# The up products of the last block as seven products of halves, on four streams and eight banks

## Chip, cores and metric

The kernel runs on one core of a Trainium2 chip. The metric is the device time of one execution in microseconds (us), as the median of several runs. The engines named below are PE (TensorE, matmuls; PEld is its weight load), DVE (VectorE), ACT (ScalarE), POOL (GpSimd) and SP (SyncE, which here only issues DMAs).

## What is computed

An attention with normalised queries and keys, followed by a gated feed-forward block (SwiGLU):

```python
q_n, k_n = rmsnorm(q, g_q), rmsnorm(k, g_k)        # 8 batches, 12 heads, 448 tokens, 64 wide
attn = softmax(q_n @ k_n.T / 8)
x = (attn @ v), heads side by side                 # 3584 x 768
g, val = x @ w_gate, x @ w_val                     # both 768 x 1536
out = (silu(g) * val) @ w_out                      # 1536 x 768
```

All of it is float32. The change touches only `x @ w_gate` and `x @ w_val`, the "up" products, of a quarter of the tokens.

## The kernel before

**Blocks and stages.** The eight batches are taken two at a time, as four blocks, `n` = 0 to 3. A block has an up stage (gate and value products), then a down stage (the product with `w_out`). Attention of the next block's tokens is interleaved with the down stage of blocks 0 to 2; block 3 has no attention beside it.

**Fifteen products.** A block's `x` is seen as 2 x 3 blocks (two batches, three thirds of the 768 columns), and a weight as 3 x 3 blocks. Their product is done with 15 block products instead of 18. Each product `x` of `UP_ORDER` needs one sum of `x` blocks (kept in the tile `xs`, two 128-row chunks of 448 tokens, made by `sides`, L1191) and one sum of weight blocks (made once by `convert` and kept in DRAM as `up_sides`, loaded as `ws` by `load_sides`, L1417). The products go to five chains, and each is read from PSUM as soon as it is done: by a copy on ACT (COPY, L1409) or an addition or subtraction on DVE (L1411 to L1415) into one of six running sums `t0`, `t1`, `d`, `t3`, `t4`, `t5`. `UP_READ` says which; a third entry names the outcome (0 to 5) which that read completes. The outcomes are completed at steps 7, 10, 11, 12, 13 and 14 of the 15.

**Groups.** The up stage of a block has four groups `g` (a quarter of the hidden width each). A group is 15 steps, a step is a gate product and a value product (`which` = 0 and 1), a product is two chunks of 128 rows with 448 columns. In the profile each float32 matmul shows as two records, so a product is four records and a group 120. Gate products use the two PSUM banks `mm`, value products the two banks `at`, in turn. When an outcome is complete, ACT takes silu of the gate (`gate`, L1551, from SBUF `gt` into a PSUM tile `st`), and DVE multiplies by the value (`weigh`, L1554, back into `gt`). The product with `x` = 0 is followed by one more DVE sum, `add_d` (L1528).

**The down stage** has 15 products as well, each of two halves `s` over all four groups (L1663). `combine` (L1612) makes their operands from `gt`: products 6 and 1 come first and their operands, in the tile `hs`, are made group by group (L1185 and L1189 `hs`), after outcomes 0, 1 and 4 of that group. The third product's operand is one wide sum over all groups (L1185, 1792 columns).

**The order of the work** is made when the program is built: every piece is added to a list with an engine, a duration, a due time `when`, a `rank`, the pieces that it comes after, and the buffers that it takes or uses. `Order.run` (L432) then takes, for each free engine, the piece with the smallest key `when - rank` among those that can start first. On the chip each engine runs its pieces in the order so fixed, and waits on semaphores. PSUM reads have rank 60, `combine` has rank 0 and is due when its group ends. Pieces marked `port` (sums of SBUF operands on DVE and POOL) are laid one after the other. `read`, `emit` and the like are the closures that issue a piece. `begin[g]` in the change is the due start of group `g`.

The lines that set the edge between the up and the down stage:

```python
for g in range(NG):
    when = start + 30 * (g + 1) * unit + 1.0
    before = [down_done.get(n - 1)] + ([staged[HS]] if n == 0 else [])
    combine(6, a1, a2, None, when, [hidden[g, 0], hidden[g, 1], *before], g)
    combine(1, b2, h0, ALU.subtract, when, [made[6][g], hidden[g, 4], *before], g)
combine(10, h1, b1, None, block_end(n) + 3.0, [*all_hidden, *made[1], up_done[n]])
```

## Time and profile before

| | |
|---|---|
| median of 3 runs | 1455.47 us (1453.88 to 1456.11) |
| span of the profiled execution, first to last instruction | 1452.0 us |
| up stage of block 3 | 1173.8 to 1354.2 us |
| down stage of block 3 | 1354.2 to 1444.6 us, then the last reads and stores |
| HBM traffic | 157.29 MB read, 34.60 MB written |

The profile comes from one execution of its own; only its span is known, and the runs are measured apart from it. A row of the windows view has the stretch in us, its length, then for PE, PEld, DVE, ACT and POOL the busy us and the number of records, then the granted clock of TensorE (1.00 is full), the share of the DMA engines that is busy, and GB/s. A row of the timeline has start, length (of several merged records where it ends in x and a number above 1), engine, line, operation, the tiles written and read, and in brackets the idle time before it with what ended it. A row of the groups view has line, engine, operation, tiles, shapes and count, then busy us and mean ns of one, then the idle time before them. A row of the chain of work that ended last has start, length, engine, tile, line and count.

### The profile page before, as it was taken

What the parts mean: (1) busy time and instruction counts of PE and PEld (TensorE: products, weight loads), DVE (VectorE), ACT (ScalarE), POOL (GpSimd) and SP (SyncE); (2) the same over time, 40 slices, a digit from 0 to 9 for tenths busy, and PEclk for the clock granted to TensorE, in tenths of its full rate; (3) what the DMA queues carried; (4) which work ended last, traced back from release to release, by engine and by line L of the source; (5) the groups of instructions that cost most, each with busy time, mean ns of one, the idle gap of its engine ahead of it and who ended that gap; (6) DMA issues with size and microseconds to landing.
All of it is one profiled execution on the core that took longest, in us unless ns stands there. A gap on an engine that the chain in (4) does not pass through costs nothing.

```text
span 1452.0 us, 19362 instructions
## 1 busy us (share of the span) xinstructions
PE 1426.0 (98%) x6736; PEld 689.5 (47%) x6736; DVE 879.8 (61%) x1485; ACT 601.6 (41%) x1210; POOL 405.7 (28%) x476
## 2 busy tenths in 40 slices
PE   8999999999999999999999999999999999999997
PEld 4455454534444455544444455544444445555553
DVE  5889876878866434546877642455686644442533
ACT  6875444476653222356564122345555322212100
POOL 4756666625443000022443200011434300000000
PEclk9999999999999999999999999999999999999999
DMA  7778979854643533433644623443463452322235
GB/s 196 217 219 268 352 266 310 260 149 90 129 103 64 133 102 92 114 113 70 122 98 86 138 74 107 107 112 93 85 126 77 95 135 73 108 73 90 69 100 110
DMA packets 410416, 193.29 MB, mean 133 GB/s; under 512 B 280004, under 2 KB 390852, under 8 KB 410308
## 3 DMA queue, kind: packets, MB, share of 16 engines
q1 hardware_dynamic: 399040, 190.57, 49.1%
q10 hardware_dynamic: 11140, 1.38, 0.7%
q8 instruction: 55, 0.90, 0.3%
q14 instruction: 53, 0.43, 0.1%
q0 software_dynamic: 128, 0.00, 0.0%
HBM read 157.29 MB, written 34.60 MB: 132 GB/s over the span
## 4 chain that ended last, share of the span: by engine, by line
PE 90%; DMA 3%; DVE 2%; ACT 2%; SPq 1%; issue 1%; POOL 1%; ACTq 0%; DVEq 0%; POOLq 0%
PE at L1474 25%; PE mm L1474 25%; PE mm L1663 23%; PE at L1049 8%; PE st L970 7%; PE st L1080 1%; PE mm L1080 1%; DMA out_dram<-spare 1%; SPq L768 1%; DMA work<-in_k_dram 1%; ACT es L985 1%; DMA xs<-in_moe_w_gate_dram 0%; PE st L908 0%; DMA v<-in_v_dram 0%; ACT work L918 0%
## 5 line engine op out<-in xcount | busy, mean ns | idle before, releaser
L1474 PE MATMUL at<-xs,ws 128*128 128x448 f32 x960 | 401.2, 540 | 2.5 <-DVE v L1413 1.4
L1474 PE MATMUL mm<-xs,ws 128*128 128x448 f32 x960 | 401.7, 541 | 0.2 <-DVE hs L1315 0.2
L1474 PEld LDWEIGHTS at<-xs,ws 128*128 128x128 f32 x960 | 181.4, 190 | 184.7 <-issue 166.7
L1474 PEld LDWEIGHTS mm<-xs,ws 128*128 128x128 f32 x960 | 182.2, 190 | 180.7 <-issue 177.9
L888 POOL TENSOR_TENSOR work<-work,rr 128x448 f32<-128x448 f32 x72 | 71.8, 1016 | 467.5 <-DVE rr L715 341.6
L1663 PE MATMUL mm<-gt,ws 128*128 128x448 f32 x448 | 175.5, 543 | 0.0
L970 PE MATMUL st<-work 64*64 64x448 f32 (+1 forms) x1536 | 151.2, 501 | 10.3 <-ACT work L918 4.9
L985 ACT ACTIVATE es<-st 128x896 f32<-128x896 f32 x129 | 114.2, 914 | 101.6 <-PE at L1049 87.8
L1411 DVE TENSOR_TENSOR gt<-gt,mm 128x448 f32<-128x448 f32 x64 | 39.7, 621 | 188.1 <-PE mm L1474 161.7
L1663 PE MATMUL mm<-hs,ws 128*128 128x448 f32 x384 | 151.3, 544 | 0.0
L990 POOL TENSOR_TENSOR sums<-es 128x896 f32<-128x896 f32 x36 | 77.2, 2145 | 176.8 <-PE st L1080 83.7
L1663 PEld LDWEIGHTS mm<-gt,ws 128*128 128x128 f32 x448 | 83.6, 190 | 83.0 <-issue 80.8
L1551 ACT ACTIVATE st<-gt 128x448 f32<-128x448 f32 x96 | 52.3, 547 | 159.1 <-DVE gt L1415 85.7
L1409 ACT COPY gt<-mm 128x448 f32<-128x448 f32 x80 | 42.6, 532 | 157.5 <-PE mm L1474 157.4
L1049 PE MATMUL at<-es,v 64*64 64x448 f32 (+1 forms) x1032 | 106.0, 507 | 0.0
L1663 PEld LDWEIGHTS mm<-hs,ws 128*128 128x128 f32 x384 | 71.3, 190 | 71.0 <-issue 70.1
L970 PEld LDWEIGHTS st<-work 64*64 64x64 f32 x1536 | 50.9, 133 | 79.1 <-issue 37.4
L1409 ACT COPY v<-at 128x448 f32<-128x448 f32 x96 | 51.0, 532 | 80.4 <-PE at L1474 79.6
L990 POOL TENSOR_TENSOR sums<-sums,es 128x896 f32<-128x896 f32 x36 | 76.0, 2112 | 2.8
L1049 PEld LDWEIGHTS at<-es,v 64*64 64x64 f32 (+1 forms) x1032 | 44.1, 134 | 56.2 <-issue 50.4
L1554 DVE SCALAR_TENSOR_TENSOR gt<-st,v 128x448 f32<-128x448 f32 x96 | 59.7, 622 | 7.3 <-DVE v L1415 0.5
L1411 DVE TENSOR_TENSOR v<-v,at 128x448 f32<-128x448 f32 x64 | 39.8, 621 | 39.6 <-PE at L1474 39.5
(170 smaller groups left out, 1550.5 us busy)
## 6 DMA issues: line engine op xcount, KB each, us to landing
ws<-up_sides SPq DMA_DIRECT2D x32, 1024.0 KB, 5.6
ws<-down_sides SPq DMA_DIRECT2D x16, 1024.0 KB, 5.7
ws<-down_sides SPq DMA_DIRECT2D x28, 512.0 KB, 4.8
ws<-up_sides SPq DMA_DIRECT2D x16, 768.0 KB, 4.9
out_dram<-spare SPq DMA_DIRECT2D x168, 56.0 KB, 2.1
v<-in_v_dram SPq DMA_DIRECT2D x96, 96.0 KB, 2.5
ws<-up_sides SPq DMA_DIRECT2D x32, 256.0 KB, 5.9
ws<-up_sides SPq DMA_DIRECT2D x16, 512.0 KB, 5.8
```

The costliest lines, as they stand in the source:

```text
L888: nc.gpsimd.tensor_tensor(out=tiles["t", m][:, x], in0=tiles["qk", (m, x)], in1=rr.to_broadcast([P, NC, C]), op=ALU.mult,)
L970: nc.tensor.matmul(st[ds(D * x, D), h, 0:n], tiles["KT", m][rows, ds(P * j + D * of_keys, D)], tiles["QT", m][rows, ds(Q * of_queries, n)] ...
L985: nc.scalar.activation(e, tiles["st", (m, j)][:, :, 0 : S * width(j) // P], AF.Exp)
L990: nc.gpsimd.tensor_tensor(out=to, in0=tiles["e", (m, 0)] if j == 1 else to, in1=e, op=ALU.add)
L1049: nc.tensor.matmul(tiles["at", (m, x)][ds(D * h, D), ds(0, Q) if early else queries], tiles["v", m][rows, j, h], tiles["e", (m, j)][rows, ...
L1080: nc.tensor.matmul(to[ds(D * h + C * x, C)], halves[:, x] if half else many[:, 0:C], term[:, h, 0:Q] if half else term[:, h, ts(x, Q)], st ...
L1409: nc.scalar.copy(to, ps)
L1411: nc.vector.tensor_tensor(out=to, in0=old, in1=ps, op=ALU.add)
L1474: nc.tensor.matmul(ps(), w[:, which, c, at], xs[:, SLOT[x], c], start=fresh and c == 0, stop=c == NC2 - 1, skip_group_check=True,)
L1551: nc.scalar.activation(take(*act, [P, 2, TB])[:, 0, 0:S], to, AF.Silu)
L1554: nc.vector.scalar_tensor_tensor(to, tiles[act][:, 0, 0:S], 1.0 / SCALE, tiles[ready], op0=ALU.mult, op1=ALU.mult,)
L1663: nc.tensor.matmul(banks[s][:, 0:S], w[:, s, g, at], where[x][:, g], start=fresh and g == 0, stop=g == NG - 1, skip_group_check=True,)
```

## The change

In block 3 the groups 1, 2 and 3 compute each of the 15 products in another way. The 448 tokens are cut into two halves (A1, A2), the 256 rows into the two chunks, and gate and value weight are taken as the two columns of one matrix. That 2 x 2 by 2 x 2 product of blocks is then done with seven products of 224 columns (Winograd's form) instead of eight:

- `halves_of` makes, on POOL during group 0, four sums of halves for each of the 15 operands: S3 (in place of A21), S2, S1 and S4. S1 lies in `hs`, S2 in `work`, S4 in `es`.
- `prepare` makes the seven weight sides out of the four, for three products at a time: a load from `up_sides` into `e` or `t`/`QT` buffers, four POOL sums of 384 columns, and a store into the new DRAM tile `up7`. Eight of these are laid into the up stage of block 1, seven into that of block 2, due every 16 us.
- `sevens` runs the three groups as one run of 45 steps with four streams: X, Y and Z are two half products each, side by side in one bank, W is one. Z and W lag two steps behind. X uses the banks `mm`, Y the banks `at`, Z and W the two `st` tiles of two banks each. Each stream is read into its own running sums just as before, and only the six outcomes are put together: four half sums on POOL (X into itself, X into Y, Y into X, Y into itself), `sow` (X is added to Z in `gt`; on POOL, in the last group on DVE), `top` (W is added to the left half of Y, DVE), then silu in place in `gt` (ACT) and `weigh` (DVE).
- The loads of the three groups take three products at a time, in pieces of 12 (X, Y) and 9 (Z, W) blocks of 128 columns.
- `combine` waits for the last product of stream Y, which still reads `hs`.
- The first piece of the down stage's weights goes into the `qk` buffers; the down stage's two banks swap if the count of groups asks for it; `UP_SUMS` is put in another order, so that three products' sides lie side by side.

The core of the diff:

```diff
+    SEVEN = {3: (1, 2, 3)}
+    HALF, LAG = S // 2, 2
+    up7 = {
+        g: dram.tile([P, 5, 7, 3, P], F32, name=f"up7_{g}")
...
+    SHORT = 40.0
+
+    def up_time(n, g=NG):
+        return sum(SHORT if i in SEVEN.get(n, ()) else 30 * PRODUCT for i in range(g))
...
+    PREPARE, PREPARE_PACE, up7_done = {1: [(g, u) for g in (1, 2, 3) for u in range(5)][:8], 2: [(g, u) for g in (1, 2, 3) for u in range(5)][8:]}, 16.0, {}
...
+        def halves_of():
+            for step, x in enumerate(UP_ORDER):
+                before = [old_done[x], *side_done[n, x], down_done.get(n - 1), clusters[EARLY * (n + 1) - 1, "total"]]
+                for i, (to, one, two, op) in enumerate((
+                    ("S3", "A11", "A21", ALU.subtract), ("S2", "A22", "S3", ALU.subtract),
+                    ("S1", "S2", "A11", ALU.add), ("S4", "A12", "S2", ALU.subtract),
+                )):
+                    done = order.add(
+                        "POOL", 0.55, begin[seven[0] - 1] + (2 * step + 2) * unit + 0.6 * i,
...
+        PARTS = dict(
+            X=((0, "A11"), (3, "S2")), Y=((2, "S1"), (1, "S3")),
+            Z=((0, "A12"), (2, "A22")), W=((1, "S4"),),
+        )
...
+            for k in range(15 * len(seven) + LAG):
+                for stream in "XYZW":
+                    j = k - LAG * (stream in "ZW")
+                    if 0 <= j < 15 * len(seven):
+                        steps.append((now, stream, j // 15, j % 15))
+                        now += q * len(PARTS[stream])
...
+                    for side, (slot, of) in enumerate(PARTS[stream]):
+                        nc.tensor.matmul(
+                            half(ps(), side), w[:, slot, at], part_of(of, x),
+                            start=fresh and side == 0, stop=True, skip_group_check=True,
+                        )
...
+                if stream == "Y":
+                    hs_free = third_done[x] = last
...
+                closing = "DVE" if j == len(seven) - 1 else "POOL"
+                if stream == "X":
+                    ready7["X"] = plus(Xr, Xr, Xl, when + 1.0, [done], [kx])
+                elif stream == "Y":
+                    u4 = plus(Yl, Xr, Yl, when + 1.0, [done, ready7["X"]], [kx, ky])
+                    u3 = plus(Xr, Xr, Yr, when + 1.7, [u4], [kx, ky])
+                    ready7[g, result] = u3, plus(Yr, Yl, Yr, when + 2.4, [u3], [ky])
+                elif stream == "Z":
+
+                    def sow(tile_at=tile_at, t=t, g=g, result=result, engine=closing):
+                        to = gt[:, g, result]
+                        eng = nc.gpsimd if engine == "POOL" else nc.vector
+                        eng.tensor_tensor(out=to, in0=to, in1=tile_at("X", t), op=ALU.add)
...
+                    def top(tile_at=tile_at, t=t):
+                        to = half(tile_at("Y", t), 0)
+                        nc.vector.tensor_tensor(out=to, in0=to, in1=tile_at("W", t), op=ALU.add)
...
+                    def weigh(g=g, result=result, tile_at=tile_at, t=t):
+                        to = gt[:, g, result]
+                        nc.vector.scalar_tensor_tensor(
+                            to, to, 1.0 / SCALE, tile_at("Y", t), op0=ALU.mult, op1=ALU.mult,
+                        )
...
+                    hidden[g, result] = order.add(
+                        "DVE", 0.62, when + 2.0, weigh, after=[gated, done], uses=[ky], port=True,
+                    )
...
+                for i, (to, one, two) in enumerate(((2, 1, 0), (3, 5, 2), (1, 5, 1), (6, 4, 3))):
+                    done = order.add(
+                        "POOL", 0.92, when + 8.0 + i,
...
         for g in range(NG):
-            when = start + 30 * (g + 1) * unit + 1.0
-            before = [down_done.get(n - 1)] + ([staged[HS]] if n == 0 else [])
+            when = begin[g + 1] + 1.0
+            before = [hs_free, down_done.get(n - 1)] + ([staged[HS]] if n == 0 else [])
```

More of the change, by code (lines that the diff above doesn't have):

```diff
@@ L1419, in load_sides @@
         n = 2 * (NC2 if sums is UP_SUMS else NG)
-        to = take(*key, [P, WS])[:, 0 : n * len(part) * P]
+        if key[0] == "qk":
+            tiles[key] = work
+        else:
+            take(*key, [P, WS])
+        to = tiles[key][:, 0 : n * len(part) * P]
         to = to.rearrange("p (n x f) -> p n x f", n=n, f=P)
@@ L1441, in block @@
         start = block_start(n)
-        unit = (block_end(n) - start) / (30 * NG)
+        unit = PRODUCT + MORE * (n == 0) / (30 * NG)
+        begin = [start + (30 * g * unit if n == 0 else up_time(n, g)) for g in range(NG + 1)]
+        seven = SEVEN.get(n, ())
         last = down_done.get(n - 1)
@@ L1454, in up_product @@
             nonlocal last
-            when = start + (2 * (15 * g + step) + which) * unit
-            b = ("BCDAE".index(CHAIN[x]) % 2 if CHAIN[x] != "E" else 0) ^ (g % 2) ^ (n > 0)
+            when = begin[g] + (2 * step + which) * unit
+            b = ("BCDAE".index(CHAIN[x]) % 2 if CHAIN[x] != "E" else 0) ^ flips[g]
             fresh = x in FRESH
@@ new lines, in restore @@
+        def restore():
+            for step, x in enumerate(UP_ORDER):
+                side_done.setdefault((n, x), []).append(
+                    order.add(
+                        "POOL", 0.55, third_done[x]["when"] + 1.0,
+                        lambda x=x: nc.gpsimd.tensor_tensor(
+                            out=part_of("A21", x), in0=part_of("A11", x), in1=part_of("S3", x),
+                            op=ALU.subtract,
+                        ),
+                        after=[third_done[x]], port=True,
+                    )
+                )
@@ L1588, in block @@
                 up_product(g, step, UP_ORDER[step], which, load, key)
+                old_done[UP_ORDER[step]] = last
+            if seven and g == seven[0] - 1:
+                halves_of()
+        if n in PREPARE:
+            prepare()
         up_done[n] = last
@@ L1594, in block @@
             )
+        turned_over = int(NG - 1 in seven and len(seven) % 2 == 0)
         bank_read[:] = [free[0, 0], free[0, 1]]
@@ L1642, in down_product @@
             piece = step // 2
-            key = ("ws", (n, "o", piece))
+            in_qk = n == NB - 1 and piece == 0 and NG - 1 in seven
+            key = ("qk" if in_qk else "ws", (n, "o", piece))
+            rest = [("qk", (n, "o", i)) for i in range(1, BUFS["qk"])] * in_qk
             size = 2 if piece < 7 else 1
@@ L1648, in down_product @@
                     lambda: load_sides(key, down_sides, DOWN_ORDER[2 * piece :][:2], DOWN_SUMS),
-                    after=[*last_load, *(weights["down", i] for i in range(2 * NG))], takes=[key],
+                    after=[*last_load, *(weights["down", i] for i in range(2 * NG))], takes=[key, *rest],
                     moves=[
@@ L1670, in down_product @@
                 after=[
-                    last, loads[piece], bank_read[s], *made.get(x, []),
+                    last, loads[piece], bank_read[s ^ turned_over], *made.get(x, []),
                     *(all_hidden if x in (14, 0, 5, 7) else []),
                 ],
-                uses=[key], mode="full",
+                uses=[key, *rest], mode="full",
             )
```

259 lines of the change are left out of this document (248 added, 11 removed).

## Prediction

> **What bounds the kernel now.** First the span and its clock, then the page's busy shares and its chain of work, then the windows view over the stages that the change touches.
>
> ```profile
> core 0: 1452.0 us, clock 0.997
> PE 1426.0 (98%) x6736; PEld 689.5 (47%) x6736; DVE 879.8 (61%) x1485; ACT 601.6 (41%) x1210; POOL 405.7 (28%) x476
> PE 90%; DMA 3%; DVE 2%; ACT 2%; SPq 1%; issue 1%; POOL 1%; ACTq 0%; DVEq 0%; POOLq 0%
> 524.70:569.80 45.10, 45.10 (x122) 22.80 (x121) 17.18 (x28) 9.68 (x18) 0.00 (x0) 1.00 0.27 88
> 1309.20:1354.20 45.00, 45.00 (x121) 22.72 (x120) 17.18 (x28) 9.67 (x18) 0.00 (x0) 1.00 0.27 82
> 1354.20:1399.00 44.80, 44.80 (x121) 22.66 (x120) 22.80 (x17) 5.33 (x10) 0.00 (x0) 1.00 0.39 104
> 1354.38 75.18 PE mm L1663 x200
> ```
>
> TensorE bounds all of it. The three window rows are one up group of block 1, the last up group of block 3 and the first half of its down stage: PE is busy for the whole stretch, DVE for 17.2 of 45 us, POOL for nothing. So an up group is 120 matmul records, and the last row gives their pace: 75.18 / 200 = 0.3759 us for 448 columns, 45.11 us a group. The edge between up and down in block 3 has no gap:
>
> ```profile
> 1352.72 1.67 PE L1474 MATMUL at<-xs,ws 128*128 128x448 f32 x4
> 1354.22 4.30 PE L1663 MATMUL mm<-hs,ws 128*128 128x448 f32 x11
> 1355.15 0.62 DVE L1554 SCALAR_TENSOR_TENSOR gt<-st,v 128x448 f32<-128x448 f32 x1
> 1355.69 2.02 DVE L1185 SCALAR_TENSOR_TENSOR xs<-hs,gt 128x1792 f32<-128x1792 f32 x1
> ```
>
> The down product starts when the last up product has streamed, because `combine` had made its operand beforehand; only one `weigh` (L1554) and the wide sum (L1185) run after it, and that sum is wanted two products later.
>
> **Term 1, the products.** A group's 120 records of 448 columns become 15 x 7 halves x 2 records = 210 of 224 columns. Their pace is not in the trace with full weights in a steady run. The nearest rows are the 448-column pace and a run of transposes with 112 columns and 128-column weights:
>
> ```profile
> 9.50 0.93 PE L908 MATMUL st<-ident,work 112*128 112x112 f32 x8
> L908 PE MATMUL st<-ident,work 112*128 112x112 f32 x96 | 12.0, 265 | 2.1 <-POOL work L881 1.1 <-ACT es L985 0.8 <-ACT more L985 0.2
> L1474 PEld LDWEIGHTS mm<-xs,ws 128*128 128x128 f32 x960 | 182.2, 190 | 180.7 <-issue 177.9 <-DMA ws<-up_sides 0.9 <-DVE hs L1315 0.6
> ```
>
> Eight took 0.93 us, the last record itself 0.26, so one starts every (0.93 - 0.26) / 7 = 0.096. A line through 0.096 at 112 and 0.376 at 448 columns gives 0.189 at 224. Bounds: half of 0.3759 is 0.188, twice 0.096 is 0.192. I take 0.189: 210 x 0.189 = 39.7 us a group, **5.4 less, 16.2 for three groups**. The weight load's record is 0.19 long and lay wholly beside a matmul of 0.376; it now lies beside one of 0.189.
>
> The Trainium skill, TensorE: Matmul & The Clock Gate, section "Back-to-back issue gap", speaks against the change: in a stream of weight loads and matmuls it gives about 81 ns a matmul at 128 columns where the isolated gap would be 56. Were its 25 ns added to each of 630 records, that estimate would take back 15.8 us. The transposes' row shows no such addition.
>
> **Term 2, work that must keep pace inside the three groups.** PSUM reads grow from 2 to 3.5 full widths a product, and six outcomes a group each get four half-width POOL sums, one full (`sow`), a half (`top`) and `weigh`. Durations:
>
> ```profile
> 1343.90 0.62 DVE L1415 TENSOR_TENSOR gt<-mm,gt 128x448 f32<-128x448 f32 x1 [0.15 <-PE mm L1474]
> 1344.44 0.61 DVE L1554 SCALAR_TENSOR_TENSOR gt<-st,v 128x448 f32<-128x448 f32 x1
> L1711 DVE STREAM_TRANSPOSE spare<-v 128x448 f32<-128x448 f32 x24 | 15.4, 643 | 0.6
> L1124 DVE STREAM_TRANSPOSE rd<-st 128x224 f32<-128x224 f32 x37 | 15.4, 415 | 30.2 <-PE st L1080 30.1
> L1339 POOL TENSOR_TENSOR work<-work 128x128 f32<-128x128 f32 x16 | 7.3, 454 | 0.9
> L1339 POOL TENSOR_TENSOR work<-work 128x256 f32<-128x256 f32 x8 | 5.8, 729 | 29.5 <-DVE work L1315 28.7 <-PE at L1474 0.5
> 301.88 2.34 POOL L990 TENSOR_TENSOR sums<-es 128x896 f32<-128x896 f32 x1 [3.72 <-ACT es L985]
> 302.14 2.56 DVE L1528 TENSOR_TENSOR gt<-gt,w 128x448 f32<-128x448 f32 x1
> L1528 DVE TENSOR_TENSOR v<-v,v 128x448 f32<-128x448 f32 x16 | 10.9, 683 | 0.5
> ```
>
> DVE starts a full one every 0.54 (first two rows), a half one by the transposes' difference 0.23 less, 0.31. POOL: 224 columns between 0.45 and 0.73, so 0.66, about 0.73 in a chain; a full one about 1.1. The two rows at 302 show a DVE sum of two SBUF operands held for 2.5 us while a POOL sum ran: such operations exclude each other. `weigh` used to read PSUM (`st`), which POOL did not hold up; now it reads SBUF twice and joins that lock.
>
> A group then asks POOL for 6 x (4 x 0.7 + 1.1) = 23.4 and DVE for about 28 of 39.7 us: enough on the mean. But five of the six outcomes end on steps 10 to 14: POOL 5 x 3.9 = 19.5, `top`, `weigh` and the adds of `d` about 7, in one lock, 26 us that start 2 us into step 10 and end some ten steps of 2.65 later. Copies of the next group need those tiles from step 1 on and have 1.7 steps of slack in the banks; the `t4` one comes out about 0.6 late. I take **+1.0 for the two borders**, between 0 and 8 (if no read hides beneath POOL).
>
> **Term 3, the edge between up and down in block 3**, the large one. All eight `combine`s now wait for the last product of stream Y (`hs` holds S1). Behind it only Z and W of three steps are left, 18 records of 0.189, so it ends 3.4 us before the up stage's end E. And DVE's order is by key: combines of groups 0 and 1 first, then reads (rank 60), group 2, then `sow`, `top`, `weigh` by due time, and the combines of group 3, due at `begin[4]` + 1, behind all of them. From the read of product 0's Z half at E - 7.8 to the combine that lets the first down product finish, DVE has 9 full and 5 half reads, an `add_d` pair, five outcomes of `sow` (DVE here), `top`, `weigh`, and seven combines: 27 full x 0.54 + 11 half x 0.31 = 18.0, 0.6 for dependent neighbours, 2.9 for the POOL sums of the last outcome that no read hides. That ends at E + 13.7. The first down product can stream its groups 0 to 2 in the meantime (6 records, 2.25 us), so **PE stands about +11.5**. Bounds: 4.4 if that combine follows its own two outcomes at once and POOL never blocks, 17.4 if each of 12 POOL sums of 0.73 does. What is late next: the wide sum (L1185, 2.02) ends some 3 us after the start of the first product and is wanted 12 us after it, so nothing.
>
> **Term 4, the clock after that stand.**
>
> ```profile
> 290.97 1.67 PE L1474 MATMUL at<-xs,ws 128*128 128x448 f32 x4
> 295.19 0.98 PE L970 MATMUL st<-work 64*64 64x448 f32 x8 [2.56 <-ACT work L925]
> 296.11 3.07 PE L1474 MATMUL mm<-xs,ws 128*128 128x448 f32 x4
> 296.00:300.00 4.00, 4.00 (x20) 1.64 (x20) 1.61 (x4) 0.92 (x1) 1.84 (x2) 0.57 0.84 196
> ```
>
> A 2.6 us wait cost the granted clock: 0.57 over the next four us, the same four records 3.07 instead of 1.67. Price 4 x 0.43 = **1.7**; 0 if the stand is short, 3.4 if two such stretches follow.
>
> **What I cost at nothing, and its cover.** The 60 `halves_of` sums of group 0 (60 x 0.7 = 42 us of an idle POOL, 2.8 a step against PE's 3.0) stay ahead of use. The loads of the three groups bring 1.4 MB every 7.9 us, in pieces with 7.9 us to land. `prepare` puts on POOL 4 sums of about 1 us every 16 us of blocks 1 and 2, and on SP some four loads and a store, in a queue where `ws` loads have about 9 us in hand.
>
> ```profile
> ws<-up_sides SPq DMA_DIRECT2D x32, 1024.0 KB, 5.6
> GB/s 196 217 219 268 352 266 310 260 149 90 129 103 64 133 102 92 114 113 70 122 98 86 138 74 107 107 112 93 85 126 77 95 135 73 108 73 90 69 100 110
> 590.08 0.88 ACT L848 COPY ss<-ss 32x28 f32<-32x28 f32 x4
> 633.12 1.36 PE L970 MATMUL st<-work 64*64 64x224 f32 x16
> ```
>
> A piece of that size lands in 5.6 us, and 130 plus some 135 GB/s is below the 352 of the fifth slice. In block 1 `prepare` keeps `t` and `QT` until about 135 us into the block; attention's first sums stood there at 110 (590 - 480) and its first scores at 153. The chain between them takes some 11 us, so it still fits; without that cover the scores, and with them the end of that block, would be a few us late.
>
> **The sum.** 1452.0 - 16.2 + 1.0 + 11.5 + 1.7 = 1450.0 for the span. The median of the runs shown, 1455.5, lies 3.5 us above the span, so 1453.5: a gain of 16 of which the edge gives most back.
>
> **The rivals.**
> - *The edge is short* (0.26): the combine of group 3 follows its own two outcomes, or POOL blocks less. Stand 4.4, no clock loss: 1455.5 - 16.2 + 1.0 + 4.4 = 1444.7. For it: nothing but outcomes 0 and 1 is needed by that combine. Against: its due time lies behind all six `weigh`s.
> - *The lock paces the three groups* (0.16, slower): place, the steps 10 to 16 of each group; price, up to 8 us a border where the reads wait behind POOL's holds, as the `v<-v,v` row's mean of 683 against 0.62 us without POOL shows for single ones. It decides once the late `sow`s push the next group's copies past their 1.7 steps. Two borders at 4 us more than the forecast has, and 2 us at the edge: 1463.
> - *Preparation comes late in blocks 1 and 2* (0.05): the cover above fails by 4 us: 1457.5.
> - *The half-width matmul does not hide its weight load* (0.04): the next matmul waits out what the load's 0.19 leaves uncovered. If only the 0.096 of one 128-column weight pass shows at each of 630 records it is 60 us: 1514. The transposes, a matmul shorter than its load's record, speak against it. By the figure of the section of the Trainium skill named above it would be 15.8 us, an estimate, and so 1469.
> - *The products do not shrink in effect* (0.04): DVE and POOL pace the groups at 45 us and nothing is left over for the edge: about 1455.
>
> **How the numbers follow.** Forecast 0.45, alone 1449 to 1459. About 0.2% is 2.9 us, what a measurement of this kernel can tell from no change. Faster by more: the short edge 0.26 and the lower part of the forecast 0.17, together 0.43. Within: 0.27 of the forecast, the last rival's 0.04 and 0.02 of late preparation, 0.33. Slower: the lock 0.16, weight loads 0.04, late preparation 0.03 and 0.01 of the forecast, 0.24. The range 1442 to 1463 leaves out a stand of nothing at all, the worst of the lock, and the weight loads.
>
> **What would show it.** Term 1: in the windows of groups 1 to 3 a pace of 0.189 a record of 224 columns; 0.25 or more would make the prediction wrong at its root. Term 2: in the waits, PE idle on ACT copies or DVE reads at the group borders, below 2 us in all. Term 3: in the timeline one gap of 9 to 13 us within the first `mm<-hs` product, ended by DVE `hs`, with DVE solid in it; a gap below 6 is the short edge. Term 4: granted clock near 0.5 for 3 to 4 us right behind that gap. Blocks 1 and 2: first scores and block starts at the same times as before.

## The result and the profile after

The changed kernel takes 1472.98 us, the median of four runs (1469.85 to 1475.49), against 1454.68 for the kernel before on the same chip: a ratio of 1.0123, 95% interval 1.0106 to 1.014. It is slower, and 19.5 us above the 1453.5 forecast. The profiled execution took 1469.85 us; its span is 1467.7, 15.7 more than before.

The span with its clock, then the page's busy shares, then windows over the stretches shown of before (columns as there):

```profile
core 0: 1467.7 us, clock 0.990
```

```profile
PE 1421.3 (97%) x7006; PEld 743.2 (51%) x7006; DVE 926.9 (63%) x1569; ACT 614.5 (42%) x1246; POOL 569.8 (39%) x680
```

```profile
524.70:569.80 45.10, 41.33 (x106) 20.48 (x105) 13.06 (x23) 8.58 (x16) 14.46 (x15) 0.96 0.75 271
1219.00:1264.00 45.00, 44.77 (x220) 40.90 (x219) 24.67 (x44) 13.65 (x29) 21.61 (x32) 1.00 0.42 147
1264.00:1309.00 45.00, 43.05 (x223) 41.41 (x222) 32.84 (x55) 14.46 (x32) 26.21 (x33) 1.00 0.47 160
1309.00:1354.00 45.00, 40.47 (x199) 37.99 (x197) 30.88 (x53) 11.69 (x26) 22.80 (x30) 0.96 0.47 151
1354.00:1399.00 45.00, 36.25 (x84) 18.80 (x85) 26.93 (x37) 7.72 (x14) 1.20 (x2) 0.81 0.16 48
```

PE is no longer solid. It idles in block 1 (first row, 3.8 us), a little in each stretch of the sevens, and most at the start of the down stage, where the granted clock is 0.81 over 45 us. The waits view of PE (engine, tile, line, releaser: us in total, times, longest) names the places that are new:

```profile
PE mm L2026 <- DVE hs L1199: 7.3, 1, 7.3
...
PE at L1737 <- ACT spare L1424: 3.9, 3, 1.9
PE st L1737 <- DVE gt L1430: 3.9, 1, 3.9
PE mm L1495 <- DMA ws<-up_sides: 3.8, 1, 3.8
```

In the changed file L1495 is the old up product, L1737 a product of the sevens, L2026 the down product, L1447 the load of weights `ws`, L1424 ACT's copy of a bank, L1426 to L1430 DVE's reads of banks, L1199 and L1203 `combine`, L1855 `top`, L1867 `weigh`, L1863 the silu.

**Block 1, 5.7 us lost; +5.0 by the start of block 3**, as the stages around it were some 0.7 shorter than before. Timeline of SP, a line of its waits view, and one of the chain of work that ended last:

```profile
546.05 2.49 SPq L1903 DMA_DIRECT2D work<-up_sides  x4
548.70 0.48 SPq L1924 DMA_DIRECT2D up<-es  x1
549.23 2.30 SPq L1447 DMA_DIRECT2D ws<-up_sides  x2
```

```profile
SPq L1903 <- DMA up<-work: 8.3, 1, 8.3
```

```profile
549.23 8.63 DMA ws<-up_sides
```

PE's timeline behind it:

```profile
557.90 2.11 PE L1495 MATMUL mm<-xs,ws 128*128 128x448 f32 x4 [3.77 <-DMA ws<-up_sides]
559.80 3.07 PE L1495 MATMUL at<-xs,ws 128*128 128x448 f32 x4
```

`prepare` was due every 16 us, but between its stores (L1924) at 501.69 and 555.69 lie five more: one every 9 us, well ahead of the due times. A piece begins with loads (L1903) into a buffer that an earlier piece must have stored. Those at 546.05 held SP's queue for 8.3 us, until that store had landed, and behind them stood the weights that PE needed next. These were issued at 549.23. At the 15.03 us between two such issues in the kernel before they would have gone out at 539.1 (from the first at 479.00), so they were 10.1 late. They also took 8.63 us to land, 3.0 more than the 5.6 of before. Some 9.3 us were in hand, so 3.8 were missing: PE waited 3.77 us and then ran at half clock (four records in 3.07 instead of 1.67).

**The three groups**, 1224.0 to 1357.84, take 133.9 us against 135.3 before and 630 x 0.189 = 119.1 by the forecast's pace: 14.8 too long. The pace itself is as forecast (PE's timeline, four records and one alone):

```profile
1277.40 0.92 PE L1737 MATMUL st<-xs,ws 128*128 128x224 f32 x4
...
1324.89 0.35 PE L1737 MATMUL st<-xs,ws 128*128 128x224 f32 x1
```

(0.92 - 0.35) / 3 = 0.19 from record to record. Added up from gap to gap, about 0.8 of the excess is at the opening, 5.2 at the end (the 3.9 us wait and half clock behind it) and 8 at the two borders between groups; the rest is in small gaps. One border (ACT's, DVE's and PE's timelines):

```profile
1264.06 1.44 DVE L1867 SCALAR_TENSOR_TENSOR gt<-gt,spare 128x448 f32<-128x448 f32 x1
...
1270.97 0.53 ACT L1424 COPY spare<-at 128x448 f32<-128x448 f32 x1 [3.68 <-DVE gt L1867]
...
1273.47 0.55 ACT L1424 COPY gt<-st 128x448 f32<-128x448 f32 x1
1273.89 1.53 ACT L1863 ACTIVATE gt<-gt 128x448 f32<-128x448 f32 x3
...
1274.77 0.62 DVE L1426 TENSOR_TENSOR v<-v,mm 128x448 f32<-128x448 f32 x1 [2.65 <-PE mm L1737]
1275.30 0.62 DVE L1867 SCALAR_TENSOR_TENSOR gt<-gt,spare 128x448 f32<-128x448 f32 x1
...
1275.95 0.53 ACT L1424 COPY spare<-at 128x448 f32<-128x448 f32 x1 [0.54 <-DVE gt L1867]
...
1276.54 0.65 PE L1737 MATMUL at<-hs,work 128*128 128x224 f32 x2 [1.88 <-ACT spare L1424]
```

A copy of stream Y waits on ACT 3.68 us for a `weigh` to free its tile. Behind it stand further copies, and only behind those three silus. The first silu is over by about 1274.5 (0.58 us alone). The next `weigh` (1275.30) needs it, but stands on DVE behind the read of a bank (L1426), and that read waits for PE's own product until 1274.77. The next copy waits for that `weigh`, and PE for the copy. The profile's chain of work that ended last goes the same way at both borders: PE's product, DVE's read, `weigh`, ACT's copy, PE. So what sets the 1.88 us is DVE's order, a read ahead of a `weigh`; the late silus stand one link behind it. The first row is a `weigh` of 0.62 us held to 1.44 beside POOL's sums.

**The edge to the down stage** (PE's and DVE's timelines):

```profile
1355.44 1.86 PE L1737 MATMUL st<-xs,ws 128*128 128x224 f32 x4 [3.85 <-DVE gt L1430]
...
1357.84 4.16 PE L2026 MATMUL mm<-hs,work 128*128 128x448 f32 x6
...
1368.09 0.62 DVE L1867 SCALAR_TENSOR_TENSOR gt<-gt,spare 128x448 f32<-128x448 f32 x1
1368.63 0.62 DVE L1199 SCALAR_TENSOR_TENSOR hs<-gt 128x448 f32<-128x448 f32 x1
...
1369.31 7.96 PE L2026 MATMUL mm<-hs,work 128*128 128x448 f32 x13 [7.30 <-DVE hs L1199]
```

First a product of stream Z waits for a bank whose read (L1430) stands behind combines of earlier groups in DVE's order (1350 to 1354); then six records of the first down product run, for groups 0 to 2; then PE waits until the combine of group 3, which DVE makes at 1368.63, right behind the last `weigh`. From its first matmul to the end of its last (1460.3) the down stage takes 102.5 us against 90.4 before. The sum: +5.0 up to block 3, -1.4 in the groups, +12.1 in the down stage, 15.7.

### The profile page after: what moved, and what is told of

It reads as the page before. It is cut to its first block, busy times and chain, and to the rows that moved or that the text cites. A ratio compares the mean times of both kernels' runs of the same rounds, so it can differ in the third digit from the quotient of the medians.

```text
span 1467.7 us, 20459 instructions
## 1 busy us (share of the span) xinstructions
PE 1421.3 (97%) x7006; PEld 743.2 (51%) x7006; DVE 926.9 (63%) x1569; ACT 614.5 (42%) x1246; POOL 569.8 (39%) x680
## 4 chain that ended last, share of the span: by engine, by line
PE 86%; DVE 5%; DMA 4%; ACT 2%; issue 1%; SPq 1%; POOL 1%; DVEq 0%; ACTq 0%; POOLq 0%
PE mm L2026 23%; PE at L1495 20%; PE mm L1495 19%; PE at L1063 7%; PE st L984 7%; PE st L1737 3%; PE at L1737 2%; PE mm L1737 2%; PE st L1094 1%; PE mm L1094 1%; DMA work<-in_k_dram 1%; DMA out_dram<-spare 1%; ACT es L999 1%; SPq L782 1%; DMA ws<-up_sides 1%
## 5 line engine op out<-in xcount | busy, mean ns | idle before, releaser
L1495 PE MATMUL at<-xs,ws 128*128 128x448 f32 x780 | 327.6, 543 | 4.7 <-DVE v L1428 3.6
L1495 PE MATMUL mm<-xs,ws 128*128 128x448 f32 x780 | 326.0, 540 | 4.0 <-DMA ws<-up_sides 3.8
L1495 PEld LDWEIGHTS at<-xs,ws 128*128 128x128 f32 x780 | 147.7, 191 | 154.1 <-issue 135.6
L1495 PEld LDWEIGHTS mm<-xs,ws 128*128 128x128 f32 x780 | 147.7, 190 | 151.5 <-issue 143.5
L2026 PE MATMUL mm<-gt,ws 128*128 128x448 f32 x448 | 175.5, 543 | 0.0
L2026 PE MATMUL mm<-hs,ws 128*128 128x448 f32 x352 | 139.1, 545 | 0.0
L2026 PEld LDWEIGHTS mm<-gt,ws 128*128 128x128 f32 x448 | 83.6, 190 | 83.0 <-issue 81.0
L1426 DVE TENSOR_TENSOR gt<-gt,mm 128x448 f32<-128x448 f32 x52 | 32.3, 620 | 136.5 <-PE mm L1495 110.4
L2026 PEld LDWEIGHTS mm<-hs,ws 128*128 128x128 f32 x352 | 65.2, 190 | 65.1 <-issue 64.2
L1572 ACT ACTIVATE st<-gt 128x448 f32<-128x448 f32 x78 | 42.4, 546 | 125.3 <-DVE gt L1430 67.3
L1424 ACT COPY gt<-mm 128x448 f32<-128x448 f32 x65 | 34.6, 533 | 122.5 <-PE mm L1495 122.3
L1424 ACT COPY v<-at 128x448 f32<-128x448 f32 x78 | 41.4, 531 | 62.9 <-PE at L1495 62.1
L1917 POOL TENSOR_TENSOR es<-es 128x384 f32<-128x384 f32 x32 | 31.2, 998 | 75.5 <-DMA es<-up_sides 75.0
L821 ACT ACTIVATE work<-work 128x448 f32<-128x448 f32 (+1 forms) x92 | 52.0, 584 | 19.9 <-DMA work<-in_k_dram 10.7
```

What stands on the lines that cost most here:

```text
L821: nc.scalar.activation(tiles["t", m][:, x], of, AF.Square)
L1424: nc.scalar.copy(to, ps)
L1426: nc.vector.tensor_tensor(out=to, in0=old, in1=ps, op=ALU.add)
L1495: nc.tensor.matmul(ps(), w[:, which, c, at], xs[:, SLOT[x], c], start=fresh and c == 0, stop=c == NC2 - 1, skip_group_check=True,)
L1572: nc.scalar.activation(take(*act, [P, 2, TB])[:, 0, 0:S], to, AF.Silu)
L2026: nc.tensor.matmul(banks[s ^ turned_over][:, 0:S], w[:, s, g, at], where[x][:, g], start=fresh and g == 0, stop=g == NG - 1, skip_group_ch ...
```

## The experiments

All changes are to the changed kernel; times are medians, ratios are to the kernel before on the same chip.

**One price at a time.** The spread preparation:

```diff
-    for _ in range(2)], **mine,
+    for _ in range(2)], early=0.0, **mine,
...
-    after=[done], uses=keys[which], moves=[transfer(P, 84 * P)],
+    after=[done], uses=keys[which], moves=[transfer(P, 84 * P)], early=0.0,
```

> The kernel after, with the two issues of `prepare` on SP's queue (its loads and its stores) not allowed ahead of their due time, so that the prepared sums are spread over block 1 at one per 16 us and not at one per about 9 us. Theory (order of SP's queue): the weight load that PE waited for in block 1 (3.8 us) stood behind a prepared store that waited for POOL; with the stores spread, that wait and the half clock behind it (1.8 us) go, about -5 us, 1473 to about 1468. Rival (bandwidth: the prepared sums' bytes themselves delay the weights): the same bytes move, a wait of 2 us or more stays somewhere in blocks 1 or 2, 1471 to 1475.

1466.57 us, ratio 1.0081 (1.0054 to 1.0108), so 6.4 less than the changed kernel. Block 1's up stage in the windows view, with the spread preparation and, below it, without:

```profile
480.87:634.31 153.44, 153.44 (x409) 77.42 (x407) 60.95 (x102) 40.90 (x81) 33.07 (x34) 1.00 0.69 213
```

```profile
478.80:637.98 159.18, 155.41 (x409) 77.82 (x407) 65.25 (x114) 47.27 (x94) 36.73 (x38) 0.99 0.68 211
```

The same 409 records take 5.7 us less, PE without a gap, at the same 213 against 211 GB/s over the stage, and SP issues the weights every 15.03 us again. So it was not the bytes as such. The edit spreads both the loads that hold SP's queue and the traffic, and no run parts the two; the sum above does: issued in time, the weights would have been there some 6 us early even at 8.63 us of landing, while 10.1 us late they miss by 0.8 even at 5.6. The store that waits for POOL, which the expectation names, is there too (555.69), but PE did not wait for the weights behind it.

Seven products in two groups only:

```diff
-    SEVEN = {3: (1, 2, 3)}
+    SEVEN = {3: (1, 2)}
-    PREPARE, PREPARE_PACE, up7_done = {1: [(g, u) for g in (1, 2, 3) ...
+    PREPARE, PREPARE_PACE, up7_done = {1: [(g, u) for g in (1, 2) ...
```

> The kernel after, with seven products for groups 1 and 2 alone; group 3 goes back to the old form, 120 records at 0.376 us, and stands between the sevens and the down products. Theory (the price lies at the edge where the sevens' last combines are the down products' operands): PE's waits of 3.9 and 7.3 us and the clock lost around them (about 6 us) go, about -17, and one third of the gain, 5.4 us, is given back, as is one border; in sum about -10 to -13 us, 1473 to about 1461. Rival (the edge is not the price: the sevens are slow wherever they stand): only the third of the gain is lost, 1473 to about 1478.

1459.18 us, ratio 1.0028 (1.0016 to 1.004): 13.8 less, though a third of the products is given back, and a little more than the 10 to 13 expected. The edge in PE's timeline:

```profile
1355.69 1.67 PE L1495 MATMUL at<-xs,ws 128*128 128x448 f32 x4
1357.19 5.05 PE L2026 MATMUL mm<-hs,ws 128*128 128x448 f32 x13
```

No wait, and 13 records of the first down product take 5.05 us, where the same 13 took 7.96 behind the stand: 2.9 us of clock.

Another order of the last combines:

```diff
+            when_1 = when
+            if NG - 1 in seven:
+                ends = begin[seven[0]] + 45 * 7 * PRODUCT / 4
+                when = ends - (2.0 if g == NG - 1 else 48.0)
+                when_1 = ends - 0.1
             combine(6, a1, a2, None, when, [hidden[g, 0], hidden[g, 1], *before], g)
-            combine(1, b2, h0, ALU.subtract, when, [made[6][g], hidden[g, 4], *before], g)
+            combine(1, b2, h0, ALU.subtract, when_1, [made[6][g], hidden[g, 4], *before], g)
```

> The kernel after, with other due times for the last combines only: the hidden outcomes of groups 0 to 2 for the first down stream come 48 us before the sevens end, that of group 3 right behind the weighings it reads, and those of the second down stream last. Theory (VectorE's order at the edge, not its work): the 3.9 us wait near the end of the sevens goes, the 7.3 us wait falls to about 4.5 to 6 us, and with one of two falls of the clock gone about 2 to 3 us more: -8 to -11 us, 1473 to about 1463. Rival (the chain of silu, weighing and combine of group 3 sets the stand, whatever the order): the 7.3 us wait stays and at most 3 us are gained, 1470 or more.

1463.03 us, ratio 1.0061 (1.0043 to 1.0079): 9.9 less, as the theory had it. PE's timeline at the edge:

```profile
1356.81 2.52 PE L2031 MATMUL mm<-hs,work 128*128 128x448 f32 x6 [1.17 <-DVE hs L1199]
1363.28 11.73 PE L2031 MATMUL mm<-hs,work 128*128 128x448 f32 x26 [3.95 <-DVE hs L1199]
```

The 3.85 us wait is gone but for two of 0.34, the 7.30 us one is 3.95, and the six records in front run at full clock. That leaves 0.7 + 1.2 + 4.0 = 5.8 of 11.2 us: 5.3 were order. The rest is mostly group 3's own chain of `sow`, `top`, silu, `weigh` and combine, on which DVE has no gap above 0.4 us.

Keeping PE busy in the stand, with matmuls that nothing reads:

```diff
                 for g in range(NG):
+                    for _ in range(9 if n == NB - 1 and x == 6 and s == 0 and g == NG - 1 else 0):
+                        nc.tensor.matmul(
+                            banks[1 ^ turned_over][:, 0:S], w[:, s, 0, at], where[x][:, 0],
+                            start=True, stop=True, skip_group_check=True,
+                        )
```

> The kernel after, with 9 more matmuls of 448 columns ahead of the first down product that waits for group 3, into a bank that is started anew later; their results are used by nothing. They take 9 x 0.376 = 3.4 us of the 7.3 us in which PE stands there. Theory (the granted clock falls because PE stands, and this is a price of its own): the stand falls below 4.5 us, the matmuls behind it run at full clock or are slow for a shorter time, -2 to -3 us, 1473 to about 1470. Rival (the clock falls anyway, for the wait in what remains of the stand): 1472 to 1474.

1470.46 us, ratio 1.0103 (1.0069 to 1.0138), 2.5 less; the intervals of this and the changed kernel overlap, so the timeline carries the verdict:

```profile
1365.10 6.93 PE L2027 MATMUL mm<-hs,work 128*128 128x448 f32 x18
1372.55 7.78 PE L2031 MATMUL mm<-hs,work 128*128 128x448 f32 x20 [0.52 <-DVE hs L1199]
```

The expectation had mis-sized its fill: a float32 matmul is two records, so nine are 18 records and 6.9 us, nearly the whole stand. What follows then runs at full pace, 20 records in 7.78. The operand came no sooner, counted from the first wait (this profile is 3.2 us late by then). In this pair of profiles the clock alone was worth some 2.8 us. That size varies: with the spread preparation, the same two waits (3.83 and 8.58 us) cost 3.4 us of clock in all, against 6.0 in the changed kernel's profile.

**What makes the borders.** Leaving out POOL's sums in groups 1 and 2:

```diff
                     def emit():
+                        if engine == "POOL" and j < len(seven) - 1:
+                            return
...
                         to = gt[:, g, result]
+                        if engine == "POOL":
+                            return
                         eng = nc.gpsimd if engine == "POOL" else nc.vector
```

> The kernel after, which leaves out POOL's half sums and `sow` for groups 1 and 2 of the sevens, so that the outputs that use these groups are not the reference's; VectorE's, ACT's and PE's work is as before. Theory (VectorE is held by the port that POOL's sums share, 4 to 5 us a border, and by waits for POOL's sums): the border waits of PE (2.05 and 2.05 us and the small ones around them, about 6.4 us in two borders, and 1.7 us of clock) go, about -6 to -8 us, 1473 to about 1466. Rival (VectorE's own order is late, reads first, with or without POOL): the two waits of 2 us stay, 1471 to 1473.

The outputs that use these groups are then not the reference's. 1470.53 us, ratio 1.0101 (1.0084 to 1.0118), 2.5 less. ACT's, DVE's and PE's timelines at the first border (the expectation's 2.05 us is the same wait, counted from start to start of PE's records; in this file L1867 is the silu and L1871 `weigh`):

```profile
1274.69 1.53 ACT L1867 ACTIVATE gt<-gt 128x448 f32<-128x448 f32 x3
...
1275.56 0.62 DVE L1426 TENSOR_TENSOR v<-v,mm 128x448 f32<-128x448 f32 x1 [4.44 <-PE mm L1737]
...
1277.34 0.65 PE L1737 MATMUL at<-hs,work 128*128 128x224 f32 x2 [1.88 <-ACT spare L1424]
```

The rival holds: at both borders PE's wait is 1.88 us to the hundredth, with DVE idle for 4.44 us before it at this one. POOL's lock is not what sets it. The read at 1275.56 waits for PE's product, and the `weigh` comes right behind it at 1276.10, though its silu, the first of the three, was over by about 1275.3: DVE's order, reads first, as the rival has it.

Second tiles for two of the outcomes that copies wait for:

```diff
+                    if t in ("t0", "t4") and stream == "Y" and j % 2:
+                        return "v", (n, g, stream, t)
```

> The kernel after, with a second tile for the two outcomes of stream Y (t0 and t4) that PE's bank copies at each border waited for; the second tile lies in attention buffers that are free in this block. Theory (a border's wait is the chain weighing, free tile, ACT's copy, bank): PE's waits of 2.05 us at both borders fall to under 1 us each, and with the clock behind the second one -3 to -6 us, 1473 to about 1468.5. Rival (the copies would be late all the same, for ACT or VectorE is behind): PE's waits at the borders keep their length or move to the next outcome, 1472 to 1474.

Silus ahead of copies (`rank=62.0` on the silu):

```diff
-    after=[acc["gate", g, result]], mode="silu",
+    after=[acc["gate", g, result]], mode="silu", rank=62.0,
```

> The kernel after, with the six silus of each group ranked ahead of the bank copies in ACT's order, so that two or three copies at each border no longer stand ahead of a silu. Theory (ACT's order: a copy that waits for a tile holds the silu whose weighing would free the next tile): the two PE waits of 2.05 us fall to under 1 us each and the half clock behind the second one goes, -2 to -5 us, 1473 to about 1469.5. Rival (weighing is late on VectorE, whatever ACT does): the waits keep 1.5 us or more, 1472 to 1474.

1474.58 us, ratio 1.0132 (1.011 to 1.0155), and 1473.62, ratio 1.0129 (1.0114 to 1.0145): no gain from either. In the waits view the copy of Y is no longer waited for; instead, with the second tiles and with the silus first:

```profile
PE st L1737 <- ACT spare L1424: 4.9, 2, 2.5
```

```profile
PE st L1737 <- ACT spare L1424: 4.0, 2, 2.0
```

it is the copy of stream W, whose tile a `top` frees, and that `top` stands on DVE behind a `weigh` and reads of banks that wait for PE. In the silus' run the `weigh` that frees Y's tile does come right behind its silu. Each cure alone uncovers the next link, of nearly the same length.

POOL's `sow` four microseconds earlier:

```diff
-    closing, 1.02 if closing == "POOL" else 0.62, when + 1.0, sow,
+    closing, 1.02 if closing == "POOL" else 0.62, when + (1.0 if closing == "DVE" else -3.0), sow,
```

> The kernel after, with POOL's `sow` due 4 us earlier, so ahead of the half sums that stand before it in POOL's order. Theory (the outcome that sow makes is late behind half sums): the silu and weighing behind it come up to 4 us earlier and the borders lose 1 to 2 us less, 1473 to about 1471.5. Rival (POOL's order doesn't matter, its load does): 1472.5 to 1473.5.

1473.39 us, ratio 1.0113 (1.0095 to 1.0132): no gain. PE's waits for copies rose from 3.9 to 6.8 us in its profile, of the slowest of its four runs; which of POOL's sums came later for it was not followed up.

The whole chain first, that is the silus' rank and

```diff
-    after=[done, ready7[g, result][1]], uses=[ky, kw], port=True,
+    after=[done, ready7[g, result][1]], uses=[ky, kw], port=True, rank=61.0,
...
-    after=[gated, done], uses=[ky], port=True,
+    after=[gated, done], uses=[ky], port=True, rank=61.0,
```

on `top` and `weigh`, with POOL's sums and without (as above), and the silus alone without POOL:

> As the run with the silus ranked ahead of the copies, and with `top` and `weigh` ranked ahead of VectorE's reads of banks. Theory (the whole chain from silu to free tile is late by rank): both border waits go to under 1 us in all, about -6 us, 1473 to about 1467. Rival (VectorE's reads are what frees PE's banks, and they come late now): PE waits for banks read by VectorE in more places, and the time is 1473 or more.

> The kernel that leaves out POOL's half sums and `sow` for groups 1 and 2 (the outputs of these groups are not the reference's), and now with the silus ranked ahead of the copies in ACT's order. Leaving out POOL alone kept both border waits of 2.05 us; ranking the silus alone moved them to the next copy at the same length. Theory (two chains of nearly one length end at the same tiles, POOL's sums and ACT's order, and each hides the other): with both gone PE waits under 0.7 us at each border. Rival (VectorE's own tops, weighings and reads are the chain): 1.5 us or more stays at each border.

> As the run without POOL's sums and with the silus first, and with `top` and `weigh` ranked ahead of VectorE's reads. With POOL at work that order gave eight waits for VectorE's reads (5.2 us) in place of the two for copies. Theory (those reads were late for the port that POOL's sums hold): without POOL they are gone as well, under 1 us of waits in the sevens but for the end. Rival (VectorE has too much work at a border by itself): 3 us or more of waits for VectorE's reads stay.

With POOL: 1471.05 us, ratio 1.0111 (1.0095 to 1.0126). Without POOL, one run each: 1468.04 with the silus first, 1467.62 with all. The first border in PE's timeline, with POOL and all ranked first:

```profile
1263.80 0.62 PE L1737 MATMUL at<-hs,ws 128*128 128x224 f32 x2 [1.42 <-DVE spare L1430]
...
1271.23 1.02 PE L1737 MATMUL st<-xs,ws 128*128 128x224 f32 x4 [1.14 <-DVE gt L1430]
...
1278.31 0.65 PE L1737 MATMUL mm<-xs,work 128*128 128x224 f32 x2 [0.39 <-ACT v L1424]
```

and without POOL's sums:

```profile
1264.18 0.62 PE L1737 MATMUL at<-hs,ws 128*128 128x224 f32 x2 [0.27 <-DVE spare L1430]
...
1270.86 1.02 PE L1737 MATMUL st<-xs,ws 128*128 128x224 f32 x4 [0.40 <-DVE gt L1430]
...
1277.94 0.65 PE L1737 MATMUL mm<-xs,work 128*128 128x224 f32 x2 [0.38 <-ACT v L1424]
```

The silus alone, without POOL, still left a wait of 2.0 us at each border, so the theory of that run fell. With the whole chain ranked first the waits for the copies of Y and W went, and DVE's reads came late by 1.4 and 1.1 us; without POOL they are 0.3 and 0.4. So two limits lie one behind the other: first the order, on DVE above all (with POOL at work, the run of the silus first and this one differ in the ranks of `top` and `weigh` alone), then POOL's hold on DVE. The ranks on DVE without the silus' were not tried. Waits of about 1.0 us a border stay even then, near what was expected (under 1 in all) but above it.

**All together.** Three groups with spread preparation, late combines and the ranks; and two groups with spread preparation and silus first:

> Three groups, with the spread preparation, the other due times of the last combines and the silus, tops and weighings ranked first, all together. If the three prices are separate (preparation about -5 to -6, edge about -9 to -10, borders -2 to -6): 1473 less 16 to 22, 1451 to 1457. If the borders keep their price: about 1458.

> Two groups by seven products, group 3 in the old form, with the spread preparation and the silus ranked first. The sum from the runs so far: 1459.2 less 5 to 6 for the preparation, less 2 to 3 for the one border between groups 1 and 2: 1451 to 1453, so 2 to 4 us under the kernel before. If the preparation's wait comes back in another place: 1456 to 1459.

1459.22 us, ratio 1.0023 (1.0014 to 1.0033): the borders kept their price. 1454.72, ratio 0.9994 (0.9985 to 1.0003): the kernel before, and not the 1451 to 1453 expected, as the silus' rank alone had moved the border's wait (1.98 us, for the copy of W) and waits of 1.42 and 1.45 us stayed at the end of the sevens. Then two groups with the work at the end of the sevens moved into group 3's old form behind them, and that with the border's cures as well (second tiles, silus first, and of the two ranks on DVE only that of `top`):

```diff
-            when = begin[g + 1] + 1.0
+            when = begin[g + 1] + 1.0 if NG - 1 in seven or not seven or g == NG - 1 else begin[NG - 1] + 14.0 + 3 * g
...
-    closing = "DVE" if j == len(seven) - 1 else "POOL"
+    closing = "DVE" if j == len(seven) - 1 and NG - 1 in seven else "POOL"
```

> Two groups by seven products with the spread preparation, without the silus' rank, and with the work that stood at the end of the sevens moved into the old form's group 3 behind them: `sow` of the second group on POOL instead of VectorE, and the combines of groups 0 to 2 due 14 us into group 3. Theory: the two waits at that end (1.6 and 1.6 us in the run of two groups with the spread preparation) go, 1454.7 less 3 = 1451.5, under the kernel before by 0.2 to 0.3%. Rival (POOL's sow is late there and holds group 3's tiles): 1454 to 1457.

> The version of two groups with spread preparation and late combines, and at its one border both cures at once: second tiles for the two outcomes of stream Y, the silus ranked ahead of ACT's copies, and `top` (which needs no silu) ranked ahead of VectorE's reads, so that it no longer stands behind a weighing that waits for a silu. Theory (the border's wait is the order of work on ACT and VectorE and no lack of throughput): the border's 2.2 and 1.3 us of PE waits fall to 1 us or less, 1453.5 to about 1451. Rival (POOL's hold on the port sets it): 2 us or more of waits at other places of the border, 1453 to 1455.

1453.45 us, ratio 0.9988 (0.9979 to 0.9997), where 1451.5 was expected: the waits at the end are down to two of 0.34, the border kept 3.3. And 1451.46, ratio 0.9975 (0.9966 to 0.9985): the second beats both kernels, by 3.8 us against the kernel before. Its border in PE's timeline:

```profile
1257.43 0.62 PE L1737 MATMUL at<-hs,ws 128*128 128x224 f32 x2 [0.94 <-DVE spare L1430]
...
1270.54 0.65 PE L1737 MATMUL mm<-xs,work 128*128 128x224 f32 x2 [0.39 <-ACT v L1424]
```

With a wait of 0.27 before them that is 1.6 us where the run before it had 3.3; 1 or less was expected. So the order was half of it with POOL at work. That POOL's sums are what stays is likely from the runs above, and not shown for this kernel. Which of the three cures did most was not tried apart. Last, three groups with all cures:

> Three groups by seven products with every cure found: the spread preparation, the other due times of the last combines, second tiles for the middle group's two outcomes of stream Y, silus ranked first and `top` ranked ahead of VectorE's reads. Two groups with such cures took 1451.5. If the borders and the preparation are cured as they are there, the third group brings 5.4 us less of PE's work and costs the stand at the edge (4.3 us of waits in the run of three groups with the other due times) and the clock behind it: 1451 to 1454, no better than two groups. Rival (the ranks make the edge worse, for the silus and reads of group 3 crowd there): 1456 to 1459.

1456.42 us, ratio 1.0011 (1.0002 to 1.002), 5 us behind two groups; 1451 to 1454 was expected. PE's timeline:

```profile
1352.12 3.66 PE L2035 MATMUL mm<-hs,work 128*128 128x448 f32 x6 [2.38 <-DVE hs L1199]
1358.00 12.80 PE L2035 MATMUL mm<-hs,work 128*128 128x448 f32 x26 [2.22 <-DVE hs L1199]
```

4.6 us of waits, and 6 and 26 records that take 3.66 and 12.80 us instead of 2.42 and 9.94 (0.54 + 25 x 0.376): 4.1 us of clock. So 8.7 us at the edge against 5.4 that a group gains. The expectation had counted the waits and too little clock.

## Why the prediction was wrong, step by step

- **Term 1, the products: right.** The pace of a record of 224 columns is 0.19, and the weight load of 0.19 beside it shows no more; the rival of the weight load fell, and the addition named beside it in the prediction did not appear.
- **Term 2, +1.0 for the borders: the main error.** Measured about 8: some 3 us of lost time at each of two borders and 1.7 of clock. The working had summed POOL's and DVE's load and put the `t4` copy 0.6 us late. The step that failed is the overlap: it took 1.7 steps of slack as enough and did not follow the order on DVE and ACT piece by piece. A `weigh` that frees a copy's tile stands on DVE behind a read that waits for PE, and its silu behind copies on ACT. The run without POOL's sums has the same two waits of 1.88 us, so this order alone gives them; the runs with ranks show POOL's hold as the second limit. The rival "the lock paces the three groups" had the size, 8 us, but not the cause.
- **Term 3, +11.5 for the stand: right in the main, and in size partly by luck.** The combine of group 3 came last in DVE's order, at 1368.63, and ended the stand; 3.85 + 7.30 is 11.2. It fell in two parts: combines of earlier groups stood ahead of the reads of the last Z banks; the prediction had them in the sum, not as a wait of their own. From the read of product 0 (1344.54) to the end of that combine DVE took 24.7 us, not 21.5; slow records of PE filled the difference.
- **Term 4, +1.7 for the clock: too small, about 6 here.** Because the stand fell in two, the clock fell twice: 3.1 us behind the first wait (four records in 1.86 instead of 0.92, two more 0.4 late, six in 4.16 instead of 2.42), 2.9 behind the second (13 in 7.96 instead of 5.05). The bound of 3.4 was too low for this profile; that of the run with the spread preparation just kept it.
- **`prepare`, costed at nothing: 5.0 us by the start of block 3.** The cover of attention's first scores held: no wait of PE is for it. What failed is the other cover, that the `ws` loads have about 9 us in hand on SP. A due time without an `early` limit is no lower bound: the pieces ran at 9 us instead of 16, and a load that waits for an earlier store to land blocks SP's queue with PE's weights behind it, 10.1 us late. The rival on preparation had a fitting size (4), but for scores.
- **The sum with what was measured**: 1452.0 - 16.2 + 5.0 + 0.8 + 8 + 11.2 + 6 = 1466.8, of 1467.7. The median lies 5.3 above the span, not 3.5, as the profiled run was the fastest of four; that 1.8 of the miss is spread between runs.

## What to carry to other kernels

Where an in-order queue holds both work that waits (for a free buffer, or for the bounding engine's own product) and work that frees a buffer, follow the chain through each queue piece by piece: here the average load of each engine said nothing about it, and curing one link merely uncovered the next of equal length. A stage that saves time on the bounding engine is best put where another stage follows that does not need its last results: two groups with one old group behind them beat three. A planner's due time is not a limit; ask which pieces may run early, and what waits behind them in a DMA queue.

## What was not expected of the hardware

The clock's fall did not go by the length of the wait alone. Windows of the changed kernel behind the waits at the first border (1.88 us), the second border (1.88 us), and the two stands:

```profile
1276.50:1280.50 4.00, 3.96 (x21) 3.95 (x22) 2.78 (x6) 1.37 (x4) 0.00 (x0) 1.00 0.21 35
1319.50:1323.50 4.00, 3.80 (x12) 3.52 (x13) 2.07 (x4) 1.56 (x5) 0.00 (x0) 0.61 0.00 0
1357.80:1361.80 4.00, 4.00 (x7) 1.69 (x6) 3.84 (x9) 1.15 (x2) 0.00 (x0) 0.56 0.54 155
1369.30:1375.30 6.00, 6.00 (x9) 2.94 (x10) 2.63 (x2) 0.53 (x1) 0.00 (x0) 0.53 0.00 0
```

The same 1.88 us cost nothing once and 39% of four microseconds the other time. The Trainium skill, TensorE: Matmul & The Clock Gate, Part 1, says that activity is counted in a window of some 3.4 us that runs freely. That fits a price that hangs on where the wait falls, though these two waits are shorter than the idle window that its table asks for. No run here shows the window itself.

DVE's reads of banks kept 0.61 us beside POOL's sums, while `weigh` on two SBUF operands was held to 1.44: in these traces the hold reached only operations on SBUF operands.
